# All blocks of the attention weights turned by VectorE and moved within SBUF, from the ninth pair of heads on

## The chip, the cores and the metric

The kernel runs on one core of a Trainium2 chip. The time is the device time of one execution in microseconds (us); of several executions the median is told. The engines are TensorE (PE in the profile; PEld are its weight loads), VectorE (DVE), ScalarE (ACT), GpSimd (POOL) and SyncE (SP), which here issues nearly all DMA transfers.

## What is computed

An attention with a decay, and a gated feed-forward block on its output, all in float32. There are 8 batches of 8 heads, 576 positions, head width 64, model width 512.

```python
scores = scale * np.matmul(q, k.transpose(0, 1, 3, 2))
cum = np.cumsum(np.log(np.clip(f, 0.0001, 1.0)), axis=-1)
decay = cum[:, :, :, None] - cum[:, :, None, :]
scores = np.where(causal, -1000000000.0, scores + decay)
scores = scores - np.max(scores, axis=-1, keepdims=True)
attn = np.exp(scores)
attn = attn / (np.sum(attn, axis=-1, keepdims=True) + 1e-09)
x = np.matmul(attn, v)          # heads side by side: [8, 576, 512]
h = np.maximum(x @ w_in, 0.0)   # [8, 576, 1024]
u, v = h[..., :512], h[..., 512:]
v_n = (v - mean(v)) / np.sqrt(var(v) + 1e-06)
v_s = np.einsum('ts,bsd->btd', w_spatial, v_n) + b_spatial[None, :, None]
out = (u * v_s) @ w_out
```

## The kernel before

The 64 heads are taken as 32 pairs, four pairs to a batch. The first four pairs run in a prologue (`first`) whose order is fixed by hand. From then on two generators are interleaved (the loop at the end): `attention(b)` emits the four pairs of a batch and `moe(b)` the feed-forward block of the batch before. Each `yield` carries the ns of TensorE's work that was emitted, and the loop advances the two so that the fractions of `t_attn` and `t_moe` stay level. The order so traced is a priority; a planner with costs of its own orders the instructions of each engine, and each engine then works through its queue in order. `in_one_piece` keeps the matmuls of a product together and puts the waits in front of the first.

A pair P goes like this. `scores(P)` multiplies queries and keys in blocks of 128 query rows (four row blocks of 128, 256, 384 and 512 keys, for each of the two heads, in two pieces); `weigh` adds the decay and finds the minimum on VectorE (line 307), and takes the exponential on ScalarE (line 338). The sums are inverted on VectorE (lines 353, 354) and `share` scales each row block on GpSimd (line 315; by ScalarE for pairs 5 to 7). `scores_tail(P)` does the same for the last 64 query rows of both heads at once, in a tile `tl` of 128 rows and 576 keys. The weights of a pair lie in `tt[h]` and `tl`, query rows on the partitions. The product with v needs the keys on the partitions, so every 128x128 block below the diagonal (10 for each head) and the five blocks of the tail have to be turned: 25 blocks.

There are two ways to turn one. `turn_block` and `turn_tail` transpose on TensorE into PSUM (lines 415, 426), and `evac` copies the result into the tile `e_all` (`e` in the profile), by VectorE and ScalarE in turn (line 406). From pair 8 on, `moved(P)` names the block columns 0 and 1 of both heads, 14 of the 25 blocks: `move(P)` turns them by four VectorE transposes that work in squares of 32x32 (line 456) into the tile `mid`, and `send(P)` puts the squares in their places with 16 transfers from `mid` to `e_all` (line 465), issued by SP: one for each pair of 32-partition groups, each 32 partitions by four runs of 512 bytes. The other 11 blocks go by TensorE and six copies.

`attend(P)` is the product: 28 matmuls, for moved columns from runs of 32 elements (`spread`, line 491), for the others from one piece (line 483). It waits for all copies and transfers of the pair. `e_all` and `mid` exist once each: `send(P)` waits until the product of P-1 has read `e_all`, and `move(P+1)` until the transfers of P have read `mid`. In the order of `attention`, `send(P)` stands behind the product of P-1 and the loads for P and P+1 (v, queries and keys, decay rows, all on SP's queue) and ahead of the scores of P+1; the product of P comes last. The product leaves PSUM through ScalarE and VectorE (lines 510, 513), which frees its two banks, and the scores of the pair after the next use these banks too.

## Time and profile before

| | |
|---|---|
| median of 3 runs | 785.73 us (782.53 to 787.43) |
| profiled execution | 780.25 us, span 778.5 us |
| TensorE busy | 723.6 us, 93% of the span |
| VectorE, ScalarE, GpSimd busy | 461.6, 390.2, 367.7 us |
| DMA moved | 103.69 MB, mean 133 GB/s |

The profile is one execution on the chip. A group row gives a line of the kernel, an engine, an operation and the tiles it writes and reads; the mean duration of one, and the idle time of the engine ahead of them with what ended it. Durations of matmuls overlap, since they are pipelined. SPq is the queue of SP: a time there is that of issuing a transfer, not of the transfer.

### The profile page before, as it was taken

Reading aid. Unit: us, or ns where it says so; the run is one execution under the profiler, and the core shown is the slowest. Engines: PE = TensorE matmul, PEld = TensorE weight load, DVE = VectorE, ACT = ScalarE, POOL = GpSimd, SP = SyncE. Lnnn points to the kernel's source line nnn. Section 1 sums busy time; section 2 is a strip of 40 time slices with the busy share of each in tenths; the row PEclk is TensorE's granted clock in tenths of the full one; section 3 lists DMA queues with packets and bytes.
Section 4 is the critical chain, followed back from the end, with each engine's and each line's share of the span. In section 5 each row is a group of like instructions: output and inputs, shape, how many; then the busy total and the mean of one; then the engine's idle time right before and its main releaser. Section 6 shows DMA issues by size and latency. Waiting matters only on the chain.

```text
span 778.5 us, 15237 instructions
## 1 busy us (share of the span) xinstructions
PE 723.6 (93%) x4972; PEld 578.2 (74%) x4973; DVE 461.6 (59%) x1557; ACT 390.2 (50%) x1086; POOL 367.7 (47%) x683
## 2 busy tenths in 40 slices
PE   7867988799899899999989999999999999999997
PEld 3545677586687767877778777888779777898885
DVE  6896899545755556655565565755675565621242
ACT  6865587654554435544454445545465444521241
POOL 3886664414644435434464443644463454511241
PEclk9999999899999999999999999999999999999999
DMA  7855254134566664546544656556454675220002
GB/s 226 234 173 136 90 153 144 56 93 151 143 165 149 166 178 127 152 117 170 162 133 135 177 137 179 137 135 170 143 143 134 156 186 151 55 49 28 28 1 67
DMA packets 89615, 103.69 MB, mean 133 GB/s; under 512 B 10305, under 2 KB 63553, under 8 KB 89538
## 3 DMA queue, kind: packets, MB, share of 16 engines
q1 hardware_dynamic: 84946, 94.48, 44.9%
q10 hardware_dynamic: 4592, 8.26, 3.0%
q8 instruction: 39, 0.64, 0.4%
q14 instruction: 38, 0.31, 0.1%
HBM read 67.78 MB, written 9.75 MB: 100 GB/s over the span
## 4 chain that ended last, share of the span: by engine, by line
PE 49%; DMA 8%; POOL 7%; DVE 7%; ACT 7%; issue 4%; SPq 3%; ACTq 0%; POOLq 0%; DVEq 0%
PE ps L231 31%; PE sc L327 5%; DMA out_dram<-o 5%; PE sc L231 4%; PE sc L491 3%; POOL tt L315 3%; SPq L465 2%; ACT tt L338 2%; PE sc L483 2%; DMA dt<-rows_d 2%; PE tp L231 2%; PE tp L415 2%; DVE tt L307 1%; POOL vnl L773 1%; ACT o L842 1%
## 5 line engine op out<-in xcount | busy, mean ns | idle before, releaser
L338 ACT ACTIVATE tt<-tt,nm 128x384 f32<-128x384 f32 (+2 forms) x240 | 133.0, 556 | 59.7 <-DVE nm L307 57.2
L315 POOL TENSOR_SCALAR tt<-tt,sm 128x128 f32<-128x128 f32 x192 | 98.9, 534 | 44.6 <-DVE sm L354 42.8
L818 POOL TENSOR_TENSOR gl<-u,gh 128x256 fp32r<-128x256 f32 (+1 forms) x64 | 51.4, 804 | 140.4 <-ACT gh L817 117.9
L327 PE MATMUL sc<-qk_t 64*128 64x128 f32 (+3 forms) x512 | 88.4, 464 | 8.4 <-DVE nm L307 4.6
L456 DVE STREAM_TRANSPOSE mid<-tt 128x512 f32<-128x512 f32 x96 | 56.3, 623 | 49.0 <-POOL tt L315 41.9
L231 PE MATMUL ps<-sph,vnh 128*128 128x256 f32 (+1 forms) x240 | 74.8, 312 | 4.2 <-ACT o L842 2.2
L231 PE MATMUL ps<-xh,winh 128*128 128x256 f32 (+1 forms) x232 | 73.1, 315 | 4.0 <-DVE vx L763 3.5
L307 DVE CUSTOM_DVE_ANT_1 tt<-sc,dk 128x256 f32<-128x256 f32 (+1 forms) x120 | 64.5, 550 | 20.0 <-PE sc L327 18.3
L483 PEld LDWEIGHTS sc<-e,vraw 128*64 128x64 f32 x896 | 54.4, 137 | 22.8 <-issue 4.7
L231 PE MATMUL ps<-spl,vnh 128*128 128x256 f32 (+1 forms) x240 | 70.6, 294 | 0.0
L231 PE MATMUL ps<-sph,vnl 128*128 128x256 f32 (+1 forms) x240 | 70.4, 293 | 0.0
L483 PE MATMUL sc<-e,vraw 128*64 128x64 f32 (+4 forms) x896 | 65.4, 278 | 4.9 <-ACT tl L639 3.7
L327 PEld LDWEIGHTS sc<-qk_t 64*128 64x128 f32 x512 | 44.9, 189 | 32.8 <-issue 10.0
L231 PE MATMUL ps<-xl,winh 128*128 128x256 f32 (+1 forms) x232 | 68.8, 296 | 0.0
L231 PE MATMUL ps<-xh,winl 128*128 128x256 f32 (+1 forms) x232 | 68.6, 295 | 0.0
L231 PE MATMUL ps<-winh,xh 128*128 128x512 f32 x148 | 61.4, 415 | 1.9 <-ACT o L842 1.7
L817 ACT CAST gh<-u 128x256 fp32r<-128x256 f32 (+1 forms) x64 | 27.2, 430 | 67.7 <-DVE u L814 46.0
L307 DVE CUSTOM_DVE_ANT_0 tt<-sc,dk 128x128 f32<-128x128 f32 (+1 forms) x120 | 48.8, 419 | 19.2 <-PE sc L327 16.9
L231 PE MATMUL ps<-winl,xh 128*128 128x512 f32 x148 | 58.1, 393 | 0.0
L406 DVE COPY e<-tp 128x128 f32<-128x128 f32 (+2 forms) x108 | 43.2, 403 | 20.3 <-PE tp L415 17.8
L415 PE MATMUL tp<-ident,tt 128*128 128x128 f32 x252 | 46.1, 283 | 6.7 <-DVE e L406 5.0
L491 PE MATMUL sc<-e,vraw 128*64 128x256 f32 (+1 forms) x384 | 47.2, 359 | 4.7 <-DMA e<-mid 1.7
(217 smaller groups left out, 1823.1 us busy)
## 6 DMA issues: line engine op xcount, KB each, us to landing
e<-mid SPq DMA_DIRECT2D x384, 64.0 KB, 2.1
qk_t<-in_dram SPq DMA_DIRECT2D x32, 608.0 KB, 5.4
dk<-rows_d SPq DMA_DIRECT2D x58, 320.0 KB, 4.6
vraw<-in_dram SPq DMA_DIRECT2D x32, 320.0 KB, 3.6
dt<-rows_d SPq DMA_DIRECT2D x58, 144.0 KB, 4.8
out_dram<-o ACTq DMA_DIRECT2D x28, 256.0 KB, 2.9
w<-in_dram SPq DMA_DIRECT2D x16, 256.0 KB, 2.8
w<-in_dram SPq DMA_DIRECT2D x4, 512.0 KB, 5.9
```

The source lines that it names most:

```text
L231: T.matmul(o, l, r, start=st, stop=sp)
L307: return V.tensor_tensor_reduce(out=out, in0=ps, in1=dec, scale=-0.125, scalar=3.0e38, op0=ALU.add, op1=ALU.min, accum_out=acc_)
L315: G.tensor_scalar(out=t, in0=t, scalar1=r, scalar2=1.0, op0=ALU.mult, op1=ALU.mult)
L327: return lambda: T.matmul(ps[:, c:c + n], qk_t[p, n - 128:n], qk_t[p, 640:640 + n], start=True, stop=True)
L338: last["exp", P, h, i] = A.activation(t, t, AF.Exp, bias=nm, scale=-1.0, accum_out=sm)
L406: copied.setdefault(P, []).append(by(out, ps))
L415: T.transpose(out=tp[:, (i - c) * 128:(i - c + 1) * 128], in_=tt[h][:, off(P)[i] + 128 * c:off(P)[i] + 128 * c + 128], identity=ident)
L456: V.transpose(out=part(mids[0][:, h, c, 0, 32 * c:], [[32, NB - c], [128, 4], [1, 32]]), in_=part(tt[h][:, ROFF[c] + 128 * c:], [[RSTEP, N ...
L483: return lambda: T.matmul(x[64 * h:64 * h + 64, o:o + n], vt[:, c, h, :], e_all[:, e0:e0 + n], start=first, stop=c == end)
L491: return lambda: T.matmul(out, vt[:, c, h, :], src, start=c == 0, stop=c == end)
L817: A.copy(gh[j][:, 0:nt], g)
L818: G.tensor_tensor(out=gl[j][:, 0:nt], in0=g, in1=f32(gh[j][:, 0:nt]), op=ALU.subtract)
```

## The change

From pair 8 on, all 25 blocks are turned by VectorE. `move` now takes one row block: it is called behind each of the eight shares and, for the tail, behind the share of `tl` (four full blocks and one of 64 columns), so there are ten VectorE transposes in place of four. `mid` holds four runs of 800 elements per partition, one for each group of 32 key rows; a run has 10 squares' rows for each head and 5 for the tail. `send` makes 16 transfers as before, each of 32 partitions by one run of 800 elements (3200 bytes). The transposes on TensorE and the copies behind them are no longer emitted for these pairs, and all 28 matmuls of the product read runs of 32 elements (`spread`, and `spread_tail` for the tail). The pairs 4 to 7 are turned by TensorE as before. `t_attn` is set to 26300, and `tt`, `e_all` and `mid` have new sizes.

```diff
--- before.py
+++ after.py
@@ -24,8 +24,8 @@
 TL = 512
 DM = 512
 TOFF = (0, 128, 384, 768)
-RSTEP = 384
-ROFF = tuple(RSTEP * i for i in range(4))
+RUN = 800
+ROW = (0, 1, 3, 6)
 HALVES = ((0, 256), (256, 320))
 QK = 640 + S
 EOFF = (0, 640, 1280, 1088, 576)
@@ -180,7 +180,7 @@
         load64(w_v[:, r, c, :], dh[:, r, c], dl[:, r, c], raw, w[:], t[:], mark)
 
 
-    tt = [cst.tile([128, 3 * RSTEP + TL], F32, name=f"tt{h}") for h in range(2)]
+    tt = [cst.tile([128, 1280], F32, name=f"tt{h}") for h in range(2)]
     tl = cst.tile([128, 640], F32, name="tl")
     G.memset(tl[:, S:640], 0.0)
     own = {}
...
@@ -354,9 +351,10 @@
             V.reciprocal(sm[h], sm[h])
             for i in range(NB):
                 n = 128 * (i + 1)
-                t = tt[h][:, off(P)[i]:off(P)[i] + n]
+                t = tt[h][:, TOFF[i]:TOFF[i] + n]
                 share(P, t, sm[h][:, i:i + 1])
-        move(P)
+                if moved(P):
+                    move(t, i + 1, 320 * h + 32 * ROW[i])
         yield 0
 
     def scores_tail(P):
@@ -376,6 +374,9 @@
         V.tensor_scalar(out=sm[:, 0:1], in0=sm[:, 0:1], scalar1=1.0e-9, scalar2=None, op0=ALU.add)
         V.reciprocal(sm[:, 0:1], sm[:, 0:1])
         share(P, tl[:, 0:S], sm[:, 0:1])
+        if moved(P):
+            move(tl, NB, 640)
+            V.transpose(out=part(mids[0][:, 0, 768:], [[RUN, 2], [1, 32]]), in_=part(tl[:, TL:], [[32, 2], [1, 32]]))
         yield 0
 
     warm = []
@@ -385,19 +386,15 @@
             mm(warm[0], zm[:, 0:128], zm[:, 0:512], True, True)
 
     nev = [0]
-    e_all = cst.tile([128, 3456], F32, name="e", tag="e")
+    e_all = cst.tile([128, 4 * RUN], F32, name="e", tag="e")
 
     def moved(P):
 
-        return (0, 1) if P >= 2 * PPB else ()
+        return P >= 2 * PPB
 
     def place(P, h, c, tail=False):
 
-        if not moved(P):
-            return 1600 * h + EOFF[c] + (512 - 128 * c if tail else 0)
-        if c < 2 and not tail:
-            return 1024 * h + 512 * c
-        return 2048 + 704 * h + (384 + 64 * c if tail else 256 * (c - 2))
+        return 1600 * h + EOFF[c] + (512 - 128 * c if tail else 0)
 
     copied = {}
 
...
@@ -431,13 +428,12 @@
 
     def tail_sets(P):
 
-        return ((3, 4) if moved(P) else (4, 3)), (0, 1, 2)
+        return (4, 3), (0, 1, 2)
 
     def transposes(P, h):
         for c in range(NB):
-            if c not in moved(P):
-                turn_block(P, h, c)()
-                yield 107 * (NB - c)
+            turn_block(P, h, c)()
+            yield 107 * (NB - c)
 
     def part(t, steps):
 
@@ -445,26 +441,20 @@
 
     mids = []
 
-    def move(P):
-
-        tt, _ = turn(P)
-        if moved(P) and not mids:
-            mids.append(cst.tile([128, 2, 2, 4, 128], F32, name="mid", tag="mid"))
-            G.memset(mids[0][:, :, 1, :, 0:32], 0.0)
-        for c in moved(P):
-            for h in range(2):
-                V.transpose(out=part(mids[0][:, h, c, 0, 32 * c:], [[32, NB - c], [128, 4], [1, 32]]),
-                            in_=part(tt[h][:, ROFF[c] + 128 * c:], [[RSTEP, NB - c], [32, 4], [1, 32]]))
+    def move(t, n, at):
+
+        if not mids:
+            mids.append(cst.tile([128, 4, RUN], F32, name="mid", tag="mid"))
+            G.memset(mids[0][:, 2:4, 768:RUN], 0.0)
+        V.transpose(out=part(mids[0][:, 0, at:], [[32, n], [RUN, 4], [1, 32]]),
+                    in_=part(t, [[128, n], [32, 4], [1, 32]]))
 
     def send(P):
 
-        if moved(P):
-            to = e_all[:, 0:2048].rearrange("p (k g w) -> p k g w", k=4, g=4)
-            for g in range(4):
-                for r in range(4):
-                    copied.setdefault(P, []).append(SY.dma_start(
-                        out=to[32 * r:32 * r + 32, :, g, :],
-                        in_=mids[0][32 * g:32 * g + 32, :, :, r, :].rearrange("p h c w -> p (h c) w")))
+        for g in range(4):
+            for r in range(4):
+                copied.setdefault(P, []).append(SY.dma_start(
+                    out=e_all[32 * r:32 * r + 32, RUN * g:RUN * g + RUN], in_=mids[0][32 * g:32 * g + 32, r, :]))
 
     def transposes_tail(P):
         for cs in tail_sets(P):
@@ -486,24 +476,27 @@
         def spread(x, m0, c, h, end):
             k0 = max(m0, c)
             n = m0 + 2 - k0
-            src = part(e_all[:, place(P, h, c) + 32 * k0:], [[128, 4], [32, n], [1, 32]])
+            src = part(e_all[:, 320 * h + 32 * (ROW[k0] + c):], [[RUN, 4], [32 * (k0 + 1), n], [1, 32]])
             out = part(x[64 * h:64 * h + 64, 128 * (k0 - m0):], [[32, 4], [128, n], [1, 32]])
             return lambda: T.matmul(out, vt[:, c, h, :], src, start=c == 0, stop=c == end)
+
+        def spread_tail(x, c, h):
+            src = part(e_all[:, 2 * RUN * h + 640 + 32 * c:], [[RUN, 2], [1, 32]])
+            out = part(x[64 * h:64 * h + 64, 256:], [[32, 2], [1, 32]])
+            return lambda: T.matmul(out, vt[:, c, h, :], src, start=False, stop=c == NB)
 
         for c in range(NB + 1):
             for x, s0, q0, q1, end in ((x1, 256, max(256, 128 * c), S, NB), (x0, 0, 128 * c, 256, 1)):
                 if c > end:
                     continue
-                if c in away:
-                    jobs += [spread(x, s0 // 128, c, h, end) for h in range(2)]
-                elif away and c < NB:
-                    jobs += [product(x, q0 - s0, place(P, h, c) + q0 - 128 * c, TL - q0, c, h, end, False)
-                             for h in range(2)]
-                if away and end == NB:
-                    jobs += [product(x, TL - s0, place(P, h, c, True), S - TL, c, h, end, False) for h in range(2)]
-                elif not away:
+                if not away:
                     jobs += [product(x, q0 - s0, place(P, h, c) + q0 - 128 * c, q1 - q0, c, h, end, c == 0)
                              for h in range(2)]
+                    continue
+                if c < NB:
+                    jobs += [spread(x, s0 // 128, c, h, end) for h in range(2)]
+                if end == NB:
+                    jobs += [spread_tail(x, c, h) for h in range(2)]
         in_one_piece(jobs, copied.pop(P))
         yield 2950
         for ps, s0, n in ((x0, 0, 256), (x1, 256, 320)):
...
@@ -711,12 +704,14 @@
             if nxt:
                 list(prep(P + 1))
                 mask(P + 1)
-            send(P)
-            for h in range(2):
+            if moved(P):
+                send(P)
+            for h in () if moved(P) else range(2):
                 yield from transposes(P, h)
             if nxt:
                 yield from scores(P + 1)
-            yield from transposes_tail(P)
+            if not moved(P):
+                yield from transposes_tail(P)
             if nxt:
                 yield from scores_tail(P + 1)
             yield from product(P)
@@ -844,7 +839,7 @@
             (SY if p0 == 0 and b == B - 1 else A).dma_start(out=out[bb, tok:tok + np_, :], in_=o[p0:p0 + np_, :])
 
 
-    t_first, t_attn, t_moe = 37000.0, 31000.0, 52500.0
+    t_first, t_attn, t_moe = 37000.0, 26300.0, 52500.0
 
     def step(gen, done, t):
         try:
```

The parts left out replace `off(P)` by `TOFF` in five places (the offsets of the row blocks in `tt`).

## Rows read from the trace of the kernel before

**Rows 1.** The page's first part (busy us, share of the span and instructions of each engine) and the line of the 40 equal slices that gives the granted clock of TensorE in tenths.

```profile
PE 723.6 (93%) x4972; PEld 578.2 (74%) x4973; DVE 461.6 (59%) x1557; ACT 390.2 (50%) x1086; POOL 367.7 (47%) x683
PEclk9999999899999999999999999999999999999999
```

**Rows 2.** Busy time by stretches of the span. Columns: stretch (us from the start), its length, then busy us (and instructions) of TensorE, its weight loads, VectorE, ScalarE and GpSimd, granted clock, share of the DMA engines, GB/s.

```profile
245.00:333.40 88.40, 81.74 (x579) 65.79 (x577) 53.04 (x185) 42.46 (x124) 42.15 (x83) 1.00 0.58 151
422.00:507.00 85.00, 83.31 (x592) 66.12 (x588) 50.15 (x177) 41.84 (x119) 40.98 (x80) 1.00 0.57 153
507.00:590.40 83.40, 82.35 (x600) 66.94 (x598) 53.11 (x182) 43.67 (x125) 37.55 (x74) 1.00 0.56 149
```

**Rows 3.** Instructions of TensorE in order of time around three transposes. Columns: start us, us, engine, line, operation, tiles, shape, count.

```profile
511.15 0.49 PE L415 MATMUL tp<-ident,tt 128*128 128x128 f32 x3
511.39 0.36 PE L231 MATMUL ps<-sph,vnh 128*128 128x256 f32 x1
511.60 0.28 PE L231 MATMUL ps<-spl,vnh 128*128 128x256 f32 x1
511.71 0.28 PE L231 MATMUL ps<-sph,vnl 128*128 128x256 f32 x1
```

**Rows 4.** Groups by line, operation and shape. Columns: count, busy us and mean ns of one, idle us of the engine just before them and what ended it. The first two are the transposes of VectorE, the next three the copies out of PSUM behind transposes of TensorE, the last two the shares on GpSimd (the sixth with its four shapes together).

```profile
L456 DVE STREAM_TRANSPOSE mid<-tt 128x512 f32<-128x512 f32 x48 | 34.1, 710 | 49.0 <-POOL tt L315 41.9 <-DMA dt<-rows_d 3.8 <-DMA e<-mid 2.4
L456 DVE STREAM_TRANSPOSE mid<-tt 128x384 f32<-128x384 f32 x48 | 25.7, 536 | 0.0
L406 DVE COPY e<-tp 128x384 f32<-128x384 f32 x48 | 26.0, 541 | 2.9 <-PE tp L426 2.2 <-PE tp L415 0.6
L406 DVE COPY e<-tp 128x128 f32<-128x128 f32 x56 | 15.9, 283 | 17.3 <-PE tp L415 17.2
L406 ACT COPY e<-tp 128x256 f32<-128x256 f32 x84 | 30.8, 366 | 21.0 <-PE tp L415 14.9 <-PE tp L426 5.7
L315 POOL TENSOR_SCALAR tt<-tt,sm 128x128 f32<-128x128 f32 x192 | 98.9, 534 | 44.6 <-DVE sm L354 42.8
L315 POOL TENSOR_SCALAR tl<-tl,sm 128x576 f32<-128x576 f32 x29 | 21.9, 756 | 2.4 <-DVE sm L377 1.6
```

**Rows 5.** Groups by shape, as above: the matmuls of the product with 256 columns, read in runs of 32 (line 491) and in one piece (line 483).

```profile
L491 PE MATMUL sc<-e,vraw 128*64 128x256 f32 x288 | 39.2, 388 | 4.7 <-DMA e<-mid 1.7 <-DVE u L814 1.5 <-DVE e L406 1.1
L483 PE MATMUL sc<-e,vraw 128*64 128x256 f32 x128 | 19.5, 379 | 0.0
```

**Rows 6.** DMA issues. The first three: issuing queue, operation, tiles, count, shortest, median and longest time of one issue in ns, first and last start. The last two, from the page: KB of one transfer and median us from issue to landing.

```profile
L465 SPq DMA_DIRECT2D e<-mid x384: 585/599/2158, 187.8 to 687.6; - x192
L252 SPq DMA_DIRECT2D dt<-rows_d x58: 450/561/1297, 19.6 to 646.9; - x58
L250 SPq DMA_DIRECT2D dk<-rows_d x58: 326/371/1662, 18.6 to 645.8; - x58
e<-mid SPq DMA_DIRECT2D x384, 64.0 KB, 2.1
vraw<-in_dram SPq DMA_DIRECT2D x32, 320.0 KB, 3.6
```

**Rows 7.** A stretch of two us in which only transfers from mid to e run; columns as in rows 2.

```profile
431.00:433.00 2.00, 2.00 (x12) 1.63 (x11) 0.29 (x1) 0.70 (x3) 0.00 (x0) 1.00 0.50 105
```

**Rows 8.** Order of time: first matmuls of a product (line 491; the first and the last of 24 begin and end the list), shares of the tail (line 315, tl) and first transposes of the main part on VectorE (line 456), with the idle time before them where there is some. Columns as in rows 3.

```profile
203.23 0.65 PE L491 MATMUL sc<-e,vraw 128*64 128x256 f32 x4
242.94 0.65 PE L491 MATMUL sc<-e,vraw 128*64 128x256 f32 x4
249.05 0.75 POOL L315 TENSOR_SCALAR tl<-tl,sm 128x576 f32<-128x576 f32 x1
259.59 0.65 PE L491 MATMUL sc<-e,vraw 128*64 128x256 f32 x4 [1.46 <-DVE u L814]
568.84 1.17 DVE L456 STREAM_TRANSPOSE mid<-tt 128x512 f32<-128x512 f32 x2
574.27 0.75 POOL L315 TENSOR_SCALAR tl<-tl,sm 128x576 f32<-128x576 f32 x1
609.41 1.17 DVE L456 STREAM_TRANSPOSE mid<-tt 128x512 f32<-128x512 f32 x2 [1.17 <-POOL tt L315]
610.07 0.65 PE L491 MATMUL sc<-e,vraw 128*64 128x256 f32 x4
615.86 0.75 POOL L315 TENSOR_SCALAR tl<-tl,sm 128x576 f32<-128x576 f32 x1 [0.70 <-DVE sm L377]
628.52 0.65 PE L491 MATMUL sc<-e,vraw 128*64 128x256 f32 x4 [0.51 <-DMA e<-mid]
646.84 1.17 DVE L456 STREAM_TRANSPOSE mid<-tt 128x512 f32<-128x512 f32 x2 [1.03 <-DMA e<-mid]
696.11 0.65 PE L491 MATMUL sc<-e,vraw 128*64 128x256 f32 x4
```

**Rows 9.** Waits. The first two: who waited for whom, us in total, times, longest. The third, of TensorE's transposes of the tail (line 426): what ended the idle time before them, us and times. The fourth: the transposes of VectorE from 205 to 677 us, columns as in rows 4.

```profile
POOL dk L278 <- DMA dk<-rows_d: 49.6, 18, 12.2
DVE mid L456 <- POOL tt L315: 41.9, 31, 4.8
  POOL tl L315: 7.8, 7
L456 DVE STREAM_TRANSPOSE mid<-tt 128x512 f32<-128x512 f32 x92 | 54.0, 623 | 47.7 <-POOL tt L315 40.5 <-DMA dt<-rows_d 3.8 <-DMA e<-mid 2.4
```

More of the change, by code (lines that the diff above doesn't have):

```diff
@@ L285, in mask @@
                             pattern=[[-1, 64]], channel_multiplier=1)
-    def off(P):
-        return ROFF if P >= PPB else TOFF
     def prep_v(P):
@@ L335, in weigh @@
         n = 128 * (i + 1)
-        t = tt[:, off(P)[i]:off(P)[i] + n]
+        t = tt[:, TOFF[i]:TOFF[i] + n]
         freed[m] = lowest(t, ps[:, c:c + n], decay(dk, i), nm)
@@ L415, in turn_block @@
             T.transpose(out=tp[:, (i - c) * 128:(i - c + 1) * 128],
-                        in_=tt[h][:, off(P)[i] + 128 * c:off(P)[i] + 128 * c + 128], identity=ident)
+                        in_=tt[h][:, TOFF[i] + 128 * c:TOFF[i] + 128 * c + 128], identity=ident)
         e0 = place(P, h, c)
@@ L566, in spread @@
                 for h in range(2):
-                    t = tt[h][:, off(X)[i]:off(X)[i] + 128 * (i + 1)]
+                    t = tt[h][:, TOFF[i]:TOFF[i] + 128 * (i + 1)]
                     share(PPB + 1 if by_a else 0, t, s_[:, h, 0:1])
```

## The prediction

> **What bounds the kernel now.** I read the busy table first: TensorE is busy 723.6 us of a span of 778.5, VectorE 461.6, and the granted clock of TensorE stands at its upper level, 2.4 GHz, in nearly every slice [rows 1]. A mean says little here, so next I cut the span into stages between the products of the attention pairs. From 205 to 677 us, where the pairs that the change touches run beside the feed-forward work, TensorE idles 1 to 7 us of each 83 to 89 us stage; VectorE is busy 50 to 53 of them, ScalarE about 43, GpSimd about 40 [rows 2]. So in these stages what TensorE no longer has to do shortens the run, unless a wait opens. After 700 us no attention is left, and before about 180 us no touched pair has begun; neither part changes. The third view is the order of time on TensorE around a transpose, the fourth the groups by form, for prices, the fifth the queue of SP and the list of who waits for whom, for the deadlines.
>
> **What leaves TensorE.** Each touched pair (24 of them) loses 6 transposes of blocks and 5 of the tail, 11 in all. The duration in the trace, some 0.28 us, overlaps its neighbours, so I take spacing. Three transposes start at 511.15, the second matmul behind them at 511.60; matmuls of 256 columns follow each other every 0.12 us, which puts the end of the transposes' claim at 511.48 [rows 3]: 0.33 us for three, 0.11 each. 11 x 0.11 x 24 = **29 us off**. What hid nothing there hides nothing now: TensorE is the bound in those stages.
>
> **What leaves VectorE and ScalarE.** Six copies out of PSUM per pair, turn about: three of 256 columns on ScalarE (0.366 each, 1.10 us) and 128, 128 and 384 on VectorE (0.283, 0.283, 0.541: 1.11 us) [rows 4].
>
> **What VectorE gets.** Now it turns two blocks of 512 and two of 384 elements per pair (0.710 and 0.536: 2.49 us) [rows 4]. Then it turns 128, 256, 384, 512 for each head, 512 and 64 for the tail. No row shows the small ones; the two sizes give 0.174 us per 128 and 0.014 fixed, so 0.188, 0.362 and 0.10. The lower end is that line; the upper is a VectorE copy out of PSUM of 128 elements, 0.283, and so at most 0.5 us more per pair. By the line, which comes from the same instruction, the total is 2 x 1.80 + 0.81 = 4.40 us; VectorE does 4.40 - 2.49 - 1.11 = 0.80 us more per pair. Its stage goes from 53 to about 56 busy of 79 us, so I cost this at nothing; the cover is its idle third. If that cover is gone, it is 0.80 x 24 = 19 us.
>
> The Trainium skill (VectorE: DVE Perf Modes, Rules for kernel authors) advises TensorE for a 128x128 transpose wherever PSUM will do as its destination. The rows above price engine time the other way: 1.21 + 1.11 + 1.10 us leave three engines, 1.91 come to one. Were the rule to hold here, VectorE would be the bound and the 19 us would be lost; that is the third rival.
>
> **The product.** All 28 matmuls of a pair now read runs of 32 columns. The trace has both kinds at 256 columns: 0.388 us in runs, 0.379 contiguous [rows 5]. Four main ones per pair change kind: 4 x 0.009 x 24 = **1 us on**. Of the 10 tail ones no row in runs exists: nothing is the lower end, the same 0.009 (2 us more) the upper; I take nothing, since 64 columns are only two runs.
>
> **The transfers.** Sixteen per pair as before, 100 KB in place of 64, rows of 3200 bytes in place of 512. SP needs 0.599 us to issue one now; the nearest rows with fewer than 128 partitions (dt, 64) take 0.561, the cheapest (dk) 0.326 to 0.371 [rows 6]. I take 0.56, for the partition count is the likeness, and 0.33 and 0.60 as ends: 16 x 0.56 = 9.0 us. While only these transfers run, the engines are 0.50 busy at 105 GB/s [rows 7], so 210 GB/s when busy, and 100 KB take 0.49 us: the issue still sets the pace. Landing is 2.1 us for 64 KB and 3.6 for 320 KB of vraw [rows 6]; between them 2.3 for 100 KB, ends 2.1 and 3.6.
>
> **The wait that is moved.** The transfers of pair P start after the last transpose into mid. Until now that was a block of the main part, and the tail had most of a period in hand. Now the tail is in it: score, minimum, exponential, reciprocal, the share on GpSimd (tl), two transposes of 0.81 us, then 16 issues with one load of v between them (0.54), then landing: 0.81 + 9.0 + 0.54 + 2.3 = 12.7 us from the end of tl's share to a free product. The product of P must not come earlier. Products start 24 times from 203.23 to 696.11, so every 21.4 us [rows 8]; without the transposes every 20.2. I set each of the 21 gaps that show a share against it: next product minus end of tl's share minus 12.7 minus 1.2. Four are short: that from 242.94 to 259.59 with a share that ends at 249.80 by 4.1, that from 610.07 to 628.52 (616.61) by 2.0 [rows 8], and two by 0.5 and 0.3; sum 6.9, for 23 gaps 7.6, say 8. TensorE is handed other work first where the planner sees this, so I take half, **4 us on**, ends 0 and 8. Behind the waiting transfers on SP lie the loads of v, dk, q and k, and dt; the masks on GpSimd already wait 49.6 us for dk [rows 9], and GpSimd is under half busy, so nothing is added.
>
> Behind a transpose that waits for its share on VectorE lie the subtraction that frees the product's banks and the minima of the next pair. GpSimd's order does not change. VectorE waited 41.9 us for these shares before [rows 9], and TensorE in turn 7.8 for tl's share, over all pairs [rows 9]. That last wait goes where its pair is touched; I leave it to the low end, as about 4 us.
>
> **Sum.** -29 + 1 + 4 = -24 us. The profiled execution took 780.25 us (span 778.5); it becomes 756. The median of the three runs is 785.73, 5.5 higher, and I take the same difference off it: **762 us**. The low end, with no late transfer, no dearer product and the wait for tl's share gone, is 785.7 - 29 - 4 = 753.
>
> **The rivals.**
> 1. VectorE stands longer. Ten transposes wait for ten shares in turn: the eight main ones take GpSimd 8 x 0.534 = 4.27 us and tl 0.76 [rows 4], against some 2.1 us of standing per pair now (47.7 us ahead of 92 transposes, or 23 pairs [rows 9]). Up to 2.9 us more per pair is possible; if 0.5 of it reaches TensorE through late banks, 12 us return: -12, **774 us**. For it: strict order on VectorE. Against: VectorE stands that long now and TensorE hardly notices [rows 2].
> 2. Slower: the ring of the one mid buffer. A main transpose of the next pair must wait until the transfers have landed, tl's share comes 6.2 to 7.2 us after the first main transpose (568.84 to 575.02, 609.41 to 616.61 [rows 8]), and then 12.7 us more. That is 19.4, under 20.2. With issue at 0.60, landing at 3.6 (14.6), 7.2 and 1.1 more for the added main transposes ahead of the tail it is 22.9. From 21.4 on, the present period, it makes the run slower; at 22.9 by 1.5 x 24 = 36 us, **822 us**. For it: VectorE has already been held by these transfers (1.03 us before 646.84) and a product too (0.51 us before 628.52 [rows 8]). Against: it needs nearly all upper ends at once.
> 3. VectorE sets the pace, as the rule above has it: +19, **805 us**, decided where its busy time and its standing together fill the period. They are 13.3 + 2.1 of 20.9 now and at most 13.3 + 0.8 + 5.0 = 19.1 of 20.2.
> 4. The planner's new order puts the freed slots beside other waits and nothing is won: **785 us**.
>
> **How the numbers follow.** Chances: the forecast 0.55, rival 1 0.17, rival 2 0.12, rival 3 0.07, rival 4 0.09. The forecast's own range is 753 (low end) to 768 (all 8 us of late transfers and 2 more of the product). For 8 in 10 I add rivals 1 and 4 up to 786, which leaves out 0.19: 752 to 786. What a measurement here tells from no change is about 1%, 7.9 us. Faster by more: the forecast and most of rival 1, 0.69; within: rival 4 and the rest, 0.13; slower: 0.18.
>
> **What would show it.** In the changed profile TensorE has some 260 instructions less, its busy time falls by about 29 us, and the stages shorten from 83 to 89 to near 80. Ten transposes per pair at the prices above, an issue near 0.56 and a landing near 2.3 would bear out the terms. A product that waits for the transfers for more than 0.3 us per pair, or a transpose that waits for them, shows the ring; idle TensorE released by the minima or the subtraction on VectorE shows rivals 1 and 3. The forecast is wrong if TensorE's idle time from 205 us on grows by more than some 10 us.

## The result and the profile after

The changed kernel takes 760.37 us (median of 4 runs, 759.6 to 763.27), beside 786.58 us (782.53 to 787.98, 4 runs) for the kernel before in the same comparison. The ratio is **0.968, with an interval of 0.964 to 0.973**: 26 us are won where 24 were forecast (762 us).

The profiled execution of the changed kernel took 763.27 us, its span is 761.5. It is the slowest of its four, while the profiled execution before (780.25) lies under all of those timed. So the two traces stand only 17 us apart, and what follows explains these 17 first.

From the page of the changed kernel: busy time by engine, TensorE's granted clock in 40 slices, and the moved transfers (KB of one, median us to landing).

```profile
PE 702.2 (92%) x4708; PEld 553.2 (73%) x4709; DVE 482.4 (63%) x1629; ACT 368.3 (48%) x1014; POOL 370.0 (49%) x683
...
PEclk9998999999999999999999999999999999999999
...
e<-mid SPq DMA_DIRECT2D x384, 100.0 KB, 2.2
```

Against [rows 1], TensorE has 264 instructions less (24 pairs by 11) and is busy 21.4 us less; VectorE is busy 20.8 us more, ScalarE 21.9 less, GpSimd stands as before. The 40 slices show hardly a change of the clock; the finer cut below does.

To compare like with like I take the stretch from the first to the last product of a touched pair, in both kernels. Busy time by stretches, columns as in [rows 2]. First the kernel before:

```profile
203.23:696.11 492.88, 475.32 (x3459) 387.25 (x3458) 289.68 (x1009) 239.43 (x685) 234.11 (x456) 1.00 0.55 146
```

The changed kernel, the whole stretch and then the seven pieces of 10 us in it with a granted clock under 1:

```profile
202.02:676.04 474.02, 453.64 (x3191) 362.28 (x3190) 308.87 (x1075) 217.53 (x616) 235.71 (x456) 0.99 0.67 181
...
220.00:230.00 10.00, 7.99 (x70) 6.93 (x69) 5.22 (x14) 1.62 (x4) 5.89 (x14) 0.83 0.81 218
...
300.00:310.00 10.00, 7.53 (x77) 6.28 (x75) 6.75 (x25) 4.82 (x12) 7.16 (x13) 0.99 0.61 192
310.00:320.00 10.00, 9.64 (x53) 7.38 (x54) 7.23 (x28) 5.83 (x18) 2.07 (x7) 0.84 0.52 124
...
340.00:350.00 10.00, 7.98 (x61) 5.14 (x61) 5.48 (x15) 1.75 (x4) 6.19 (x14) 0.87 0.73 212
350.00:360.00 10.00, 10.00 (x63) 8.40 (x59) 7.21 (x33) 6.75 (x21) 2.88 (x5) 0.96 0.80 212
...
490.00:500.00 10.00, 7.16 (x45) 6.96 (x44) 4.94 (x12) 1.79 (x6) 4.98 (x10) 0.88 0.40 98
500.00:510.00 10.00, 10.00 (x79) 9.44 (x78) 4.03 (x17) 5.44 (x19) 0.73 (x1) 0.95 0.35 83
```

The stretch is 18.9 us shorter. TensorE's busy time falls by 21.7 us, its idle time grows from 17.6 to 20.4. The 21.7 look short of the 29 forecast, and the clock column says where the rest is: the seven pieces together lack 1.7 + 0.1 + 1.6 + 1.3 + 0.4 + 1.2 + 0.5 = 6.8 us of full clock, so matmuls stood longer as busy. 21.7 + 6.8 = 28.5. The slots went as forecast, and this traced execution gave a part back in clock; over all executions the change doesn't (more on it at the end).

Groups by line and shape of the changed kernel, columns as in [rows 4]: the ten transposes of a pair on VectorE, then the two kinds of matmul of the product.

```profile
L449 DVE STREAM_TRANSPOSE mid<-tt 128x512 f32<-128x512 f32 x48 | 32.7, 682 | 0.6
...
L449 DVE STREAM_TRANSPOSE mid<-tt 128x384 f32<-128x384 f32 x48 | 26.5, 552 | 0.9
...
L449 DVE STREAM_TRANSPOSE mid<-tt 128x256 f32<-128x256 f32 x48 | 20.0, 417 | 1.0
...
L449 DVE STREAM_TRANSPOSE mid<-tl 128x512 f32<-128x512 f32 x24 | 16.7, 695 | 10.3 <-DMA e<-mid 4.3 <-POOL tt L312 2.1 <-POOL tl L312 1.7
...
L449 DVE STREAM_TRANSPOSE mid<-tt 128x128 f32<-128x128 f32 x48 | 14.0, 291 | 18.8 <-POOL tt L312 14.0 <-DMA qk_t<-in_dram 2.7 <-DMA e<-mid 2.0
...
L379 DVE STREAM_TRANSPOSE mid<-tl 128x64 f32<-128x64 f32 x24 | 5.2, 216 | 10.1 <-DMA e<-mid 10.1
```

```profile
L481 PE MATMUL sc<-e,vraw 128*64 128x256 f32 x384 | 55.1, 393 | 7.1 <-DMA e<-mid 7.1
...
L486 PE MATMUL sc<-e,vraw 128*64 128x64 f32 x480 | 31.1, 222 | 0.0
```

The small transposes cost more than the line through the two large ones: 0.291, 0.417 and 0.216 us for 128, 256 and 64 elements, where 0.188, 0.362 and 0.10 were taken; the upper end of 0.283 is nearly what the smallest full one took. A pair's ten come to 2 x 1.94 + 0.91 = 4.80 us, not 4.40. The product's large matmuls take 0.393 us in runs, beside 0.388 [rows 5]; the mean takes in stretches at the lower clock.

The issues of the moved transfers (shortest, median and longest time of one in ns), of the changed kernel:

```profile
L456 SPq DMA_DIRECT2D e<-mid x384: 507/591/1624, 189.1 to 672.2; - x192
```

An issue takes 0.591 us where 0.56 was taken; the landing, 2.2, is 0.1 under its estimate.

The list of waits of the changed kernel (who waited for whom, us in total, times, longest):

```profile
DVE mid L449 <- POOL tt L312: 16.1, 17, 3.0
...
DVE mid L379 <- DMA e<-mid: 10.1, 6, 2.5
...
PE sc L481 <- DMA e<-mid: 7.1, 5, 2.6
...
DVE mid L449 <- DMA e<-mid: 6.3, 5, 2.5
```

TensorE's product waits 7.1 us for the transfers, 1.7 before [rows 5]. VectorE stands 16.4 us for the transfers, which must first have read `mid`, and 16.1 us for the shares, where it stood 41.9 [rows 9].

### The profile page after: what moved, and what is told of

Same layout as the page of the kernel before. It is cut to its first block, busy times and chain, and to the rows that moved or that the text cites. A ratio compares the mean times of both kernels' runs of the same rounds, so it can differ in the third digit from the quotient of the medians.

```text
span 761.5 us, 14645 instructions
## 1 busy us (share of the span) xinstructions
PE 702.2 (92%) x4708; PEld 553.2 (73%) x4709; DVE 482.4 (63%) x1629; ACT 368.3 (48%) x1014; POOL 370.0 (49%) x683
## 4 chain that ended last, share of the span: by engine, by line
PE 45%; DMA 8%; POOL 7%; DVE 7%; ACT 7%; issue 6%; SPq 4%; ACTq 0%; POOLq 0%; DVEq 0%
PE ps L231 28%; PE sc L324 5%; SPq L456 4%; PE sc L481 4%; PE sc L231 3%; ACT tt L335 3%; POOL tt L312 3%; DMA dt<-rows_d 3%; DMA out_dram<-o 2%; PE tp L231 2%; DMA e<-mid 2%; DVE mid L449 2%; POOL vnl L768 1%; PE sc L486 1%; ACT o L837 1%
## 5 line engine op out<-in xcount | busy, mean ns | idle before, releaser
L312 POOL TENSOR_SCALAR tt<-tt,sm 128x128 f32<-128x128 f32 x192 | 100.6, 545 | 20.6 <-DVE sm L351 17.5
L449 DVE STREAM_TRANSPOSE mid<-tt 128x128 f32<-128x128 f32 x192 | 86.6, 486 | 21.4 <-POOL tt L312 14.0
L324 PE MATMUL sc<-qk_t 64*128 64x128 f32 (+3 forms) x512 | 90.1, 472 | 7.0 <-DVE xl L506 3.4
L481 PE MATMUL sc<-e,vraw 128*64 128x256 f32 (+1 forms) x576 | 67.3, 355 | 7.1 <-DMA e<-mid 7.1
L312 POOL TENSOR_SCALAR tl<-tl,sm 128x576 f32<-128x576 f32 x29 | 22.0, 759 | 76.3 <-DVE sm L375 39.5
L231 PE MATMUL ps<-winl,xh 128*128 128x512 f32 x148 | 58.3, 394 | 0.0
L503 ACT CAST xh<-sc 128x256 fp32r<-128x256 f32 x64 | 24.8, 399 | 64.7 <-PE sc L481 39.4
L768 POOL TENSOR_TENSOR vnl<-vx,vnh 128x512 fp32r<-128x512 f32 x32 | 41.4, 1297 | 26.3 <-ACT vnh L766 25.9
L231 PEld LDWEIGHTS ps<-sph,vnh 128*128 128x128 f32 x240 | 45.2, 188 | 11.7 <-ACT o L837 5.6
```

Source lines behind the costliest of these rows:

```text
L231: T.matmul(o, l, r, start=st, stop=sp)
L312: G.tensor_scalar(out=t, in0=t, scalar1=r, scalar2=1.0, op0=ALU.mult, op1=ALU.mult)
L324: return lambda: T.matmul(ps[:, c:c + n], qk_t[p, n - 128:n], qk_t[p, 640:640 + n], start=True, stop=True)
L449: V.transpose(out=part(mids[0][:, 0, at:], [[32, n], [RUN, 4], [1, 32]]), in_=part(t, [[128, n], [32, 4], [1, 32]]))
L481: return lambda: T.matmul(out, vt[:, c, h, :], src, start=c == 0, stop=c == end)
L503: last[P, s0 // 256] = A.copy(xh[:, s0:s0 + n], ps[:, 0:n])
```

## The experiments

All change the changed kernel. Each ratio is to the kernel before, timed on the same chip; 0.01 is 7.8 us. The intervals are about 0.004 to 0.005 wide on either side, so a difference of two ratios is known to some 5 us.

### The pace alone

```diff
-    t_first, t_attn, t_moe = 37000.0, 26300.0, 52500.0
+    t_first, t_attn, t_moe = 37000.0, 31000.0, 52500.0
```

> The changed kernel with t_attn set back to 31000, so that the attention of a batch is emitted ahead of its even pace and the feed-forward work trails; nothing is computed otherwise. Theory of the slots (the gain is the 264 spaces of 0.11 us that transposes took on TensorE): the pace gives at most a third of the gain, so 758 to 769 us. Theory of the pace (the new constant, not the freed engine, made the gain): back to 780 to 787 us.

762.38 us, ratio 0.972 [0.967, 0.977]. The one constant that steers the interleaving is worth nothing that can be measured; it is the changed work that wins. This run is also the reference for the next three and for `tail_back`, which have `t_attn` raised too.

### The slots on TensorE put back

`ghost` turns the same blocks on TensorE, at their former places in the order, into PSUM tiles that nobody reads; VectorE and the transfers stay as changed.

```diff
-            for h in () if moved(P) else range(2):
-                yield from transposes(P, h)
+            for h in range(2):
+                yield from ghost(P, h, (2, 3), False) if moved(P) else transposes(P, h)
...
-            if not moved(P):
-                yield from transposes_tail(P)
+            yield from ghost_tail(P, False) if moved(P) else transposes_tail(P)
```

> The changed kernel, in which TensorE again does the 11 transposes per pair at their former places, into PSUM tiles that nobody reads; no copies follow. t_attn is 31000, which is what their time adds to the emitted work. Theory of the slots: TensorE pays 24 x 11 x 0.11 = 29 us again, so 783 to 792 us. Theory of the copies (the gain came from the 144 copies out of PSUM and the waits around them, on VectorE, ScalarE and TensorE): within 6 us of the changed kernel, 758 to 767 us.

794.14 us, ratio 1.011 [1.007, 1.016]: 0.039 over the run before, 31 us, for 264 transposes, so 0.117 us each; 794 lies 2 us above the range expected of the slots and 27 above that of the copies. The forecast's 0.11 came from the spacing in [rows 3]. Busy time on the page of this run:

```profile
PE 730.5 (92%) x4973; PEld 582.5 (73%) x4973; DVE 484.4 (61%) x1629; ACT 368.9 (46%) x1014; POOL 369.3 (47%) x683
```

TensorE is busy 28.3 us more than in the changed kernel, 0.107 for each transpose, at nearly the same mean granted clock (0.983 and 0.984), and the time follows. So the gain is the slots on TensorE, as the first term has it. But the run says one thing more: with the slots back the kernel is 9 us **slower** than the one before, although the six copies of a pair are still gone. Something added by the change costs more than the copies gave back (6 to 12 us by the interval; up to some 4 of the 9 go with the clock, see the end).

### The copies put back too

As `ghost`, with a copy behind each group of ghosts into a tile that nobody reads; first by VectorE and ScalarE in turn, then all by ScalarE. The lines of the copy are shown for the blocks; for the tail they are the same with its width.

```diff
+            if copy:
+                by = (V.tensor_copy, A.copy)[(nev[0] + 1) % 2]
+                by(scrap[:, 0:n], tp[:, 0:n])
+                nev[0] += 1
```

> As the run before, and each transposed group is copied out of PSUM by VectorE and ScalarE in turn into a tile that nobody reads: all that the change took away is there again, beside all that it added. Theory of the slots: at most 5 us above the run without copies, 783 to 797 us. Theory of the copies: 15 us or more above the run without copies. Theory of VectorE's pace (its added work is hardly covered): VectorE now has 1.1 us more per pair than in the changed kernel, so at least 20 us above the run without copies.

810.24 us, ratio 1.033 [1.029, 1.037]: 17 us over the ghosts alone, which is what the theory of the copies has (15 or more).

```diff
-                by = (V.tensor_copy, A.copy)[(nev[0] + 1) % 2]
+                by = A.copy
```

> The run with the transposes and their copies put back beside the change (810 us), in which all six copies per pair are ScalarE's and none VectorE's. Theory of VectorE's load (the copies cost 16 us there because they came on top of ten transposes per pair on VectorE): back to 790 to 800 us, near the run without copies. Theory of the copies' waits (TensorE waits for its PSUM banks whoever empties them): 804 to 815 us.

802.26 us, ratio 1.024 [1.020, 1.028]: 10 us over the ghosts, 7 less than with both engines. This lies between the expectations. Busy time on the pages of the two, the mixed copies first:

```profile
PE 733.4 (91%) x4973; PEld 585.4 (72%) x4973; DVE 500.6 (62%) x1701; ACT 389.1 (48%) x1086; POOL 370.6 (46%) x683
```

```profile
PE 732.7 (92%) x4972; PEld 584.2 (73%) x4973; DVE 481.6 (60%) x1629; ACT 409.6 (51%) x1158; POOL 369.4 (46%) x683
```

And the waits of the mixed copies for each other and for the ghosts:

```profile
ACT scrap L711 <- PE tp L706: 25.5, 14, 3.5
...
DVE scrap L711 <- ACT scrap L711: 12.0, 13, 2.1
...
DVE scrap L724 <- ACT scrap L724: 8.4, 4, 3.7
```

The first row is ScalarE standing for the ghosts. The other two are of the experiment's own making: all copies write one tile, so VectorE stands 20.4 us for ScalarE's copies, which it did not in the kernel before. I take the copies' price as 10 us (ScalarE alone, none of this) to 17. That is argued: no run has both engines copy into tiles of their own, and with ScalarE alone VectorE is spared copies that it made in the kernel before. Either way it is not nothing, as the prediction had it.

`ghost_copies` has everything of the kernel before on TensorE and, but for that wait, on the copies; what it has beyond it is what the change added: 11 more blocks on VectorE, larger, later transfers, and the rest of the product read in runs. It is 26 us slower than the kernel before, 19 if the 7 us between the two variants are all of that wait. VectorE is busy 39 us more in it (500.6 against 461.6).

### VectorE's time by itself

Once the large transpose of the tail done twice, ahead of the transfers; once as often, but behind the last transpose that the transfers wait for, into a tile of its own.

```diff
             move(tl, NB, 640)
+            move(tl, NB, 640)
```

> The changed kernel with one more VectorE transpose of 512 columns per pair (the tail's, done twice into the same place): 0.70 us more per pair, 17 us in all, just ahead of the transfers. If VectorE's idle third covers its work, as the forecast has it: 758 to 766 us. If VectorE sets the pace: 772 to 779 us.

```diff
+            V.transpose(out=part(junk, [[32, 4], [128, 4], [1, 32]]), in_=part(tl, [[128, 4], [32, 4], [1, 32]]))
```

> The changed kernel with one more VectorE transpose of 512 columns per pair, as in the run that did the tail's twice, but into a tile that nobody reads and behind the last transpose that the transfers wait for. Theory of the deadline (that run lost its 10 us because the transfers began 0.7 us later): 758 to 763 us. Theory of VectorE's pace (17 us more of VectorE cost half of it wherever they stand): 767 to 773 us.

769.95 us, ratio 0.983 [0.978, 0.987], and 772.87 us, ratio 0.985 [0.981, 0.990]: 11 and 13 us slower than the changed kernel. VectorE's busy time on the two pages:

```profile
PE 704.3 (92%) x4708; PEld 557.2 (73%) x4709; DVE 497.5 (65%) x1653; ACT 368.7 (48%) x1014; POOL 368.9 (48%) x683
```

```profile
PE 699.4 (91%) x4709; PEld 552.0 (72%) x4709; DVE 501.5 (66%) x1653; ACT 369.5 (48%) x1014; POOL 371.3 (49%) x683
```

That is 15.1 and 19.1 us more, so each us on VectorE costs about 0.7 us of the run, with an uncertainty of about 0.3, though the engine idles a third of the span. `dve_more` falls between its two expectations, `dve_after` where VectorE's pace has it. Since the one behind the deadline costs as much as the one ahead of it, to within some 5 us, the transfers' start is not the main cause. The group of the score matmuls on TensorE, 205 to 670 us (count, busy us, mean ns; idle us before them and what ended it), in the changed kernel, with the transpose doubled, and with the one behind:

```profile
L324 PE MATMUL sc<-qk_t 64*128 64x384 f32 (+3 forms) x352 | 61.7, 471 | 3.3 <-DVE xl L506 3.2
```

```profile
L324 PE MATMUL sc<-qk_t 64*128 64x384 f32 (+3 forms) x352 | 63.3, 481 | 10.8 <-DVE xl L507 10.3 <-DVE nm L304 0.5
```

```profile
L324 PE MATMUL sc<-qk_t 64*128 64x384 f32 (+3 forms) x352 | 60.9, 466 | 9.3 <-DVE xl L508 8.6 <-DVE nm L304 0.5
```

The idle time that grows is that of the scores, 3.2 to 10.3 and 8.6 us, and what ends it is the subtraction into `xl`, the one that frees the product's banks. It stands on VectorE behind the transposes. That is about half of the 11 and 13 us between the medians, and more than the two traced executions lie above that of the changed kernel (spans 768.0 and 765.2 beside 761.5). Another part shows in the clock: the mean granted clock is 0.975 to 0.981 in the six executions of `dve_more`, 0.983 to 0.988 in five of `dve_after` and 0.984 to 0.990 in the four of the changed kernel. Times the span, 17, 12 and 10 us of full clock are lacking (medians). So up to 7 of the 11 us of `dve_more` go with the clock, but only 2 of the 13 of `dve_after`.

### The tail back on TensorE

`tail_back` returns the five blocks of the tail to TensorE with their two copies; the transfers carry 80 KB and no longer wait for the tail's share. (`t_attn` goes to 28440.)

```diff
-            move(tl, NB, 640)
-            V.transpose(out=part(mids[0][:, 0, 768:], [[RUN, 2], [1, 32]]), in_=part(tl[:, TL:], [[32, 2], [1, 32]]))
...
-            if not moved(P):
-                yield from transposes_tail(P)
+            yield from transposes_tail(P)
```

> The changed kernel, in which the five blocks of the tail go by TensorE and two copies again, and the 20 others by VectorE; the transfers shrink to 80 KB and no longer wait for the tail's share. t_attn 28440. Theory of the slots: 5 x 0.11 x 24 = 13 us more than the changed kernel, less at most 4 to 7 us of waits for late transfers that go, so 766 to 773 us. Theory of the ring (the late tail share before the transfers takes as much as the tail's slots give): 755 to 762 us.

773.59 us, ratio 0.986 [0.983, 0.990]: 11 us over the run with the pace alone. Its page:

```profile
PE 711.7 (92%) x4829; PEld 564.8 (73%) x4829; DVE 475.7 (62%) x1605; ACT 373.8 (48%) x1038; POOL 369.7 (48%) x682
```

120 transposes at 0.11 us are 13 us on; VectorE is busy 6.7 us less than in the changed kernel, 5 us off at 0.7; two copies per pair come back. The sum fits without any gain from the earlier start of the transfers, so the late share of the tail cost no more than these ratios can tell, some 5 us.

### A second mid buffer

```diff
-            mids.append(cst.tile([128, 4, RUN], F32, name="mid", tag="mid"))
+            for k, tag in enumerate(("mid", "mid2")):
+                mids.append(cst.tile([128, 4, RUN], F32, name="mid", tag=tag))
...
-                    out=e_all[32 * r:32 * r + 32, RUN * g:RUN * g + RUN], in_=mids[0][32 * g:32 * g + 32, r, :]))
+                    out=e_all[32 * r:32 * r + 32, RUN * g:RUN * g + RUN], in_=mids[P % 2][32 * g:32 * g + 32, r, :]))
```

> The changed kernel with two mid tiles in turn, so that a VectorE transpose never waits until the transfers of the pair before have read mid. Theory of the ring (the one mid holds VectorE, 16 us in the trace, and through it TensorE): 746 to 755 us. Theory of the slots (VectorE's standing is covered by its idle time, the transfers cost TensorE only what it waits for at the product): 756 to 763 us.

760.4 us, ratio 0.970 [0.964, 0.974]. The transposes have another buffer to write, and the time is the same. The 16 us that VectorE stands for the transfers in the changed kernel are idle time that costs nothing that these ratios can tell: its standing for a buffer had slack here, its added work had not.

### More transfers, fewer transfers

Eight more per pair, into a tile that nobody reads, ahead of the product:

```diff
+        for n in range(8):
+            copied[P].append(SY.dma_start(out=junk[32 * (n % 4):32 * (n % 4) + 32, :], in_=mids[0][0:32, n % 4, :]))
```

> The changed kernel with 8 more transfers of the same size per pair, from mid into a tile that nobody reads, and the product waits for them too: the pair is ready some 4.7 us later. By the deadlines of the forecast (gap between products minus the 12.7 us from the tail's share to the landing) nearly every gap is then short, 2.5 us on the mean: 785 to 810 us. If the transfers have room: 758 to 768 us.

809.41 us, ratio 1.033 [1.028, 1.039]: 51 us, 2.1 per pair, for a landing that is 8 x 0.59 = 4.7 us later. The first of its waits and the one of the product:

```profile
DVE mid L379 <- DMA junk<-mid: 57.9, 19, 5.7
...
PE sc L484 <- DMA junk<-mid: 7.0, 6, 1.5
```

VectorE's wait for the buffer is now the large one, 57.9 us for the tail's second transpose alone. So the ring that the second rival described is there, and its slack is less than 4.7 us: with half as many transfers again the run is slower than the kernel before. The product waits 7.0 us for transfers, no more than the 7.1 of the changed kernel, which speaks for the ring and against a late product; a second buffer beside 24 transfers was not run.

The other way, 4 of the 16 transfers left out from the tenth pair on:

```diff
-            for r in range(4):
+            for r in range(4 if P == 2 * PPB else 3):
```

> The changed kernel without 4 of the 16 transfers of a pair from the tenth pair on (the squares of the fourth group of key rows are not moved, so the product reads there what the ninth pair left): the pair is ready some 2.4 us earlier. Theory of the late transfers (they still cost TensorE the 4 to 8 us of the forecast, at the product or in the planner's order): 750 to 757 us. If they are hidden at sixteen: 758 to 763 us.

776.05 us, ratio 0.989 [0.985, 0.994]: 17 us slower with less work, which no theory had. The wait of the product fell from 7.1 to 3.7 us. Busy time by stretches, columns as in [rows 2], cut at products:

```profile
429.56:485.37 55.81, 52.86 (x348) 39.61 (x348) 37.23 (x139) 25.63 (x75) 26.74 (x55) 1.00 0.71 203
485.37:521.61 36.24, 32.98 (x234) 29.30 (x233) 17.79 (x57) 13.87 (x38) 15.44 (x28) 0.91 0.28 73
521.61:576.74 55.13, 51.85 (x345) 38.85 (x344) 37.06 (x137) 26.12 (x76) 27.21 (x54) 1.00 0.69 190
576.74:610.37 33.63, 30.09 (x226) 26.75 (x226) 17.28 (x58) 13.06 (x37) 14.89 (x28) 0.95 0.37 96
```

The second of the same two batches in the changed kernel ends with this gap:

```profile
573.02:598.15 25.13, 25.13 (x203) 22.00 (x202) 16.80 (x58) 12.23 (x36) 13.39 (x24) 1.00 0.54 149
```

Three gaps between products take 55 us together and the fourth 34 to 36 (58.3 and 31.7, then 57.0 and 25.1 in the changed kernel, from 426.00 to 598.15 us); in the long one TensorE idles 3.3 to 3.5 us and its clock falls. The two batches take 180.8 us, beside 172.2. The pairs are bunched, and the feed-forward work of the batch is left alone at the end. That is what the trace shows; that the planner does it because the product is free earlier, and that the bunching costs the 17 us, is argued, not tried. It limits what the small experiments can say: an edit that shifts a due time also shifts the order.

### Two queues, and the tail first

Half of the transfers issued by ScalarE:

```diff
-                copied.setdefault(P, []).append(SY.dma_start(
+                copied.setdefault(P, []).append((A if r % 2 else SY).dma_start(
```

> The changed kernel with 8 of the 16 transfers of a pair issued by ScalarE's queue, so that the last is issued some 4.7 us earlier. Theory of the late transfers (products wait some 7 us for them, and more is hidden in the planner's order): 748 to 757 us. Theory of the slots with the transfers hidden: 757 to 763 us. If ScalarE, which now stands in order behind the transfers' waits, holds the exponentials up: 765 us and more.

795.85 us, ratio 1.020 [1.014, 1.025]: some 40 us worse than from one queue, the last of the three expectations. Of its list of waits:

```profile
POOL dk L278 <- DMA dk<-rows_d: 137.4, 49, 14.0
...
ACT o L837 <- DMA e<-mid: 29.3, 6, 5.4
...
ACT gh L812 <- DMA e<-mid: 16.6, 4, 5.1
```

A transfer waits for the tail's transposes and for the previous product. On SP only loads stand behind that wait. On ScalarE the output copy and the cast of the gate stood behind it, 46 us in these two rows alone. The loads came late too: the masks on GpSimd wait 137.4 us for `dk`, 34.9 in the changed kernel (49.6 before [rows 9]); why they did is not shown. The Trainium skill (DMA: Bandwidth & Descriptors, Issuing engines are not separate DMA queues) says that several issuing engines save only the sequencer's time for the issue, usually small beside the transfer. Here that time was the larger part, 16 x 0.59 us against 16 x 0.49 of moving (the prediction's estimate), and spreading it still lost; the rows put it down to the order of the queue that took it over.

Last, the tail's scores of the next pair ahead of its main scores, so that its share ends early:

```diff
+            if nxt and moved(P + 1):
+                yield from scores_tail(P + 1)
             if nxt:
                 yield from scores(P + 1)
...
-            if nxt:
+            if nxt and not moved(P + 1):
                 yield from scores_tail(P + 1)
```

> The changed kernel with the tail's scores of the next pair emitted ahead of its main scores, so that the last transposes before the transfers are those of the main blocks, as in the kernel before. Theory of the late transfers: they start 1 to 3 us earlier, 750 to 757 us. Theory that the order of the two does not matter, since the sum of shares ahead of the transfers is the same: 757 to 763 us. If the tail now holds up the minima of the main part: 764 us and more.

788.25 us, ratio 1.006 [1.003, 1.010]: 30 us worse than the changed kernel. (In this kernel the tail weights of pair 7 are overwritten before they are turned; the amount of work is the same.) Of its waits:

```profile
DVE mid L379 <- DMA e<-mid: 38.2, 18, 4.2
...
PE sc L481 <- DMA e<-mid: 13.8, 6, 3.8
```

The tail's transposes now meet `mid` while the transfers of the pair ahead still read it (38.2 us, 10.1 in the changed kernel), and VectorE stands with the next pair's minima behind them. The tail at the end is the better place. No version tried beats the changed kernel by more than the intervals.

## Why the prediction was right, and where it wasn't

The forecast, 762 us, holds: the gain is 26 us where 24 were summed. Its mechanism, the slots, is shown. That the number is so near is partly luck: two terms that stood at nothing in the sum are large and nearly cancel.

- **The slots, -29.** Right. Put back alone they cost 31 us, the tail's five 11 with their copies, and busy time falls by 28.5 once the clock is allowed for. The period between products went from 21.4 to 20.6 us (474.02 / 23) where 20.2 was expected. The price came from the spacing of [rows 3], not from the duration of some 0.28 us; by durations it would have been 74 us.
- **"What leaves VectorE and ScalarE"**, counted as nothing: wrong. By the two runs with copies they are worth 10 to 17 us. The prediction took VectorE's share of them only into a net of busy time, and ScalarE's 1.10 us not at all.
- **"I cost this at nothing; the cover is its idle third"**: wrong, the step of the working that failed. An added us on VectorE costs about 0.7 of itself. The prediction's price if the cover is gone, 19 us, was for VectorE's net time at its full length. Measured, all additions, transfers and product included, cost 19 to 26 us and take back the 10 to 17 of the copies. The net, 9 us, stands where the forecast had 5 for late transfers and product. How the 9 part among VectorE, the transfers and the clock is not shown. The runs form a chain, so their parts, -31 - 17 + 26 or -31 - 10 + 19, must add up to the -22 of the run with the pace alone; the forecast's -24 had -29 and +5 in their place.
- **Net VectorE, 0.80 us per pair (19 us).** Right in sum: its busy time grew by 20.8. The small transposes were mis-sized, 4.80 us for 4.40, as the rows above show.
- **The product in runs, +1.** 0.393 and 0.222 us, where [rows 5] has 0.388 for a large one in runs; with the slots accounted for, nothing that these runs can tell is left for this term.
- **The transfers.** Issue 0.591 for 0.56, landing 2.2 for 2.3: 0.4 us per pair together.
- **Late transfers, +4 (0 to 8).** The product's wait grew by 5.4 us, inside the range. TensorE's idle time grew by 2.8 between the products and by 4.4 from 205 us to the end (24.7 to 29.1), under the 10 us that would have made the forecast wrong.
- **Rival 1**, VectorE stands longer: not for the shares, for which it stands less than before. Nor do the scores on TensorE wait longer for the banks that VectorE frees: 3.2 us for `xl`, and 3.3 in the kernel before (205 to 690 us):

```profile
L327 PE MATMUL sc<-qk_t 64*128 64x384 f32 (+3 forms) x352 | 59.4, 455 | 4.3 <-DVE xl L513 3.3 <-DVE nm L307 1.0
```

  The consequence is real once VectorE gets still more work: banks that it frees late are what `dve_more` and `dve_after` show.
- **Rival 2**, the ring: 7.1 us over 24 pairs is 0.3 per pair, just at the mark that was set for it, and transposes wait for the transfers. A second buffer changes nothing, so it doesn't set the time; eight more transfers close it.
- **Rival 3**, VectorE sets the pace, and with it the rule of the Trainium skill (VectorE: DVE Perf Modes, Rules for kernel authors) that a 128x128 transpose belongs on TensorE when PSUM will do: in this kernel the other way round, by a ratio of 0.968 with the transfers counted in. TensorE idled 17.6 of 492.9 us, and the rule's way out of PSUM costs copies. The rule isn't empty here, since VectorE's time cost 0.7 of itself.
- **Rival 4**, nothing won by the new order, fell with the result: 26 us are won, and two settings of the pace give the same time.

## What to carry over

Moving work off the engine that bounds a stage gains its slots by spacing, and putting those slots back, unread, on the bounding engine measures the gain alone. An engine that idles a third of the time is still no cover when its in-order queue holds what the bounding engine waits for next: price its added time at a good part of itself until an experiment with unread work says less, and price what it loses in the same coin. A transfer with a long wait is better issued from a queue on which nothing urgent stands behind it.

## What the hardware showed that was not expected

TensorE's clock in the middle of the busy stages. Busy time by stretches of 2 us in the changed kernel, columns as in [rows 2]:

```profile
492.00:494.00 2.00, 1.98 (x16) 1.77 (x14) 1.30 (x3) 0.00 (x0) 2.00 (x5) 1.00 0.00 0
494.00:496.00 2.00, 0.00 (x0) 0.00 (x0) 0.54 (x1) 0.19 (x1) 0.98 (x4) 1.00 0.40 91
496.00:498.00 2.00, 1.18 (x7) 1.18 (x8) 1.10 (x2) 1.03 (x3) 0.00 (x0) 0.88 0.69 160
498.00:500.00 2.00, 2.00 (x9) 2.00 (x9) 0.00 (x0) 0.17 (x1) 0.00 (x0) 0.50 0.67 158
500.00:502.00 2.00, 2.00 (x15) 2.00 (x14) 0.00 (x0) 0.45 (x2) 0.00 (x0) 0.76 0.63 150
```

The order of time on TensorE there, columns as in [rows 3]:

```profile
496.82 0.41 PE L231 MATMUL ps<-xh,winh 128*128 128x320 f32 x1 [2.84 <-ACT u L787]
497.07 0.30 PE L231 MATMUL ps<-xh,winl 128*128 128x320 f32 x1
497.21 0.31 PE L231 MATMUL ps<-xl,winh 128*128 128x320 f32 x1
...
498.00 0.47 PE L231 MATMUL ps<-xh,winh 128*128 128x320 f32 x1
498.26 0.47 PE L231 MATMUL ps<-xh,winl 128*128 128x320 f32 x1
```

TensorE stood 2.84 us for a pass of ScalarE over the feed-forward block, started again at full speed (matmuls 0.15 us apart), and then ran at its lower level, 1.2 GHz, with the same matmuls 0.26 us apart, until about 501 us. One idle time of 2.84 us thus cost some 1.7 us more at half speed (the pieces from 490 to 510 lack 1.2 + 0.5). Before, the mean of the stretch was 1.00. In the traced execution 6.8 us went that way, in four falls; the long gaps of `send_12` show the same.

The length of an idle time alone doesn't say whether the clock falls. In the same stretch of the changed kernel TensorE idled 2 us or more five times: behind 2.01, 2.44, 2.02 and 2.84 us (the next matmul at 223.82, 310.36, 347.52 and 496.82) the clock fell, behind 2.63 us (379.99) it did not, nor in the kernel before behind 2.23 and 2.34 us (210.37 and 401.91). And it differs between executions. The full clock that an execution lacks (its span times one less the mean granted clock) is 10 us at the median of the four of the changed kernel and 8 to 11 in the kernel before beside the experiments, so the change doesn't cost clock as a rule. It is 15 us in `ghost`, 20 in `ghost_copies` and 17 in `send_12` and `dve_more`, so a part of what these lose is clock behind idle times, and not only the idle times. That TensorE falls idle in such places because it has less work left to cover the waits is argued, not tried.
